# One decode block with its gradients on one core: w1 and w3 loaded first, two V buffers, seven output tiles, ScalarE's order written by hand

## The chip, the cores and the metric

The kernel runs on one core of a Trainium2 chip. The metric is the device time of one execution in microseconds (us), the median of the runs shown below. A profile is one execution recorded by the hardware profiler; its times are those of that execution. TensorE (PE) multiplies matrices, VectorE (DVE) and ScalarE (ACT) work elementwise, GpSimd (POOL) here issues the stores, SyncE (SP) the loads.

## The reference, cut to what matters

One token of a transformer block, forward and backward. The forward part is attention over a cache of 32 heads and a gated MLP, both on the same normalized row, and the kernel returns the output and the gradients for x, the K and V caches, wq, wo, w1, w3 and w2.

```python
# A: x (1,1,640), k_cache and v_cache (1,32,8192,128), wq (640,4096), wo (4096,640), all bf16
q = (xn @ wq).reshape(B, Sq, 32, 128).transpose(0, 2, 1, 3)
p = softmax(einsum("bhqd,bhkd->bhqk", q, k) * 128 ** -0.5)
o = einsum("bhqk,bhkd->bhqd", p, v)
attn = o.transpose(0, 2, 1, 3).reshape(B, Sq, 4096) @ wo
# B: w1, w3 (640,1728), w2 (1728,640)
mlp = (silu(xn @ w1) * (xn @ w3)) @ w2
out = x + attn + mlp                      # xn = layernorm(x)
# returned: out, and the gradients of sum(out * grad_out) for x, k_cache, v_cache, wq, wo, w1, w3, w2
```

A head's K and V are 8192 x 128 each, 2.10 MB; their gradients, which are outer products, are as large and are written out. Every input is read once and every gradient is written once: 151 MB each way.

## The kernel before

Heads are worked on one after the other, in groups of four (`GH`), of which there are eight (`NG`); wq is loaded for two groups at a time, wo for one. Before the heads comes the MLP, with its gradients. Each K or V of a head lies in SBUF as 128 partitions x 64 rows x 128 columns.

The order of the instructions on VectorE, SP and POOL is the order of the program (`ORDERED`). On TensorE and ScalarE a scheduler of the framework chooses it at build time. All loads of K, V and weights are issued on SP in program order, and a load waits there until its buffer is free, with all later loads behind it. All stores of large outputs are issued on POOL, again in order.

The start (lines 98 to 157): x and grad_out are loaded, then on SP the three pieces of w2, wq of the first pair of groups, wo of group 0, w1, w3, K of head 0, and V of heads 0, 1 and 2. w1 and w3 lie in buffers of K; there are three such buffers, so K of heads 1 and 2 can be loaded only after the gradients dw1 and dw3, which are written over w1 and w3, have been stored. The pieces of w2, two scratch tiles of the MLP (`diag`, `bc_sb`) and the output tiles `ot` share the pool `op` of five buffers.

`mlp_steps` (lines 415 to 503) first multiplies w2 by the gradient of the output (L427 to L423), and stops at a `yield`. Then `prep_steps(0)` runs for the first group. Then come gate and up (L441, 160 matmuls of one column), a chain of small operations on VectorE (L446 to L459), `diag` (L461), its spreading over all partitions (L470 to L476, `bc_sb`), the gradient of w2 on ScalarE (L485), the products with w1 and w3 for the gradient of x (L492, L495), and the gradients of w1 and w3 (L498), which are stored (L502).

The loop over heads works on two heads in one iteration: on head h (`c`), and on the scores of head h+1 (`n`). For n: `product(n, "S")`, K times q on VectorE (L312), summed on TensorE (L314), in two halves; `row_max`; `product(n, "DP")`, the same with V and the gradient of o; `exps`. For c: `probs`, `row_dots`, `attend` (V times probabilities on TensorE), `dscores` (with K on TensorE), and `outer`, four times: half of dV or dK. An output tile `ot` holds 32 rows of 128 columns for each partition, 1.05 MB in all; VectorE makes 24 of the rows (L321), ScalarE 8 (L325), and POOL stores the tile (L327).

`load_v(h + 3)` stands after `attend` of head h, and `load_k(h + 3)` after `dscores` of head h. In the first head of a group come `load_wq` (every second group) and `load_wo` for the next group. The buffer of `load_wo` is that of the group before, which has to be stored as dwo first.

`weights(c)` ends each head: `odq`, `om`, the transposes of this head's wq (L399) and the copy of them (L401), their product with dq (L403), and dq spread over the partitions (L406 to L409, into `dqbc`). At the last head of a group it calls `finish_wo` and `finish_wq`, which write the group's weight gradients over wo and wq on ScalarE (L273, four activations, and L279, five) and store them; some of the last groups' stores are kept in the list `late` until head 30.

`prep_steps(g)` makes q and the gradient of o for a group: five matmuls into `ps_q` and a scaled copy `qs_g` (L241), five times four transposes of wo (L248), a copy `woT` (L250) and a matmul (L252), and a copy `do_g` (L258). It is a generator; the loop calls `gap()` at set places, which runs the next part of the first generator in the list `steps`.

Of the kernel before, what the change touches and what calls it, by code (L numbers as in the profile page):

```python
# [9 lines left out]
BF16 = mybir.dt.bfloat16  # L10
# [6 lines left out]
P = 128  # L17
# [4 lines left out]
def kernel(  # L22
# [35 lines left out]
    ORDERED = {mybir.EngineType.DVE, mybir.EngineType.SP, mybir.EngineType.Pool}  # L58
# [9 lines left out]
    kvpool = ctx.enter_context(tc.tile_pool(name="kv", bufs=3))  # L68
# [3 lines left out]
    opool = ctx.enter_context(tc.tile_pool(name="op", bufs=5))  # L72
# [23 lines left out]
    with tc.manual_schedule(engines=ORDERED):  # L96
# [8 lines left out]
        def load_k(h):  # L105
            Kt = kvpool.tile([P, J, DH], BF16, name="Kt", tag="K")
            nc.sync.dma_start(Kt[:], kc[h])
            kv_tiles[h] = kv_tiles.get(h, [None, None])
            kv_tiles[h][0] = Kt

        def load_v(h):
            Vt = kvpool.tile([P, J, DH], BF16, name="Vt", tag="V")
# [26 lines left out]

        w2_parts = []  # L140
# [9 lines left out]
        w1t = kvpool.tile([P, NC, F], BF16, name="w1t", tag="K")  # L150
        nc.sync.dma_start(w1t[:], w1_v)
        w3t = kvpool.tile([P, NC, F], BF16, name="w3t", tag="K")
        nc.sync.dma_start(w3t[:], w3_v)
# [3 lines left out]
        load_v(2)  # L157
# [75 lines left out]
        def prep_steps(g):  # L233
            G_ = grp[g]
            wq_g, wo_g = G_["wq"], G_["wo"]
            ps_q = ps_w.tile([P, GH * DH], F32, name="ps_q", tag="w")
            for ci in range(NC):
                nc.tensor.matmul(ps_q[:], lhsT=XN_rep[:, ci, :], rhs=wq_g[:, ci, :],
                                 start=(ci == 0), stop=(ci == NC - 1))
            qs_g = wpool.tile([P, GH, DH], BF16, name="qs_g", tag="qs_g")  # L240
            nc.scalar.activation(qs_g[:].rearrange("p h d -> p (h d)"), ps_q[:], ACTF.Copy, scale=scale)  # L241
            G_["qs"] = qs_g
            ps_d = ps_w.tile([P, GH * DH], F32, name="ps_d", tag="w")
            for ci in range(NC + 1):
                if ci < NC:
                    ps_t = ps_w.tile([P, GH * DH], BF16, name="ps_t", tag="w")
                    for hh in range(GH):
                        nc.tensor.transpose(ps_t[:, hh * DH:(hh + 1) * DH], wo_g[:, hh, ci * P:(ci + 1) * P], ident_bf[:])  # L248
                    woT = wpool.tile([P, GH * DH], BF16, name="woT", tag="woT", bufs=2)
                    nc.scalar.copy(woT[:], ps_t[:])  # L250
                if ci > 0:
                    nc.tensor.matmul(ps_d[:], lhsT=G_rep[:, ci - 1, :], rhs=last[:],  # L252
                                     start=(ci == 1), stop=(ci == NC))
                last = woT
# [373 lines left out]
```

## Time and profile before

| | |
|---|---|
| median of the runs | 766.21 us |
| the runs | 764.54, 766.21, 769.57 us |
| the profiled execution | 767.92 us, of which its span is 765.8 us |
| busy: PE, DVE, ACT, POOL | 72%, 83%, 62%, 11% of the span |
| moved | 303.71 MB, half read and half written, mean 397 GB/s |
| granted TensorE clock, mean | 0.783 |

The span runs from the first instruction to the last event of the profile. A line of the waits says which engine and line waited for which; L312 is line 312 of the kernel before. "DMA share" is the mean busy share of the core's 16 DMA engines; it can read slightly above 1, since packets overlap. "out_dram<-ot" is the store of an output tile, "Kt<-in_A_k_cache_dram" the load of a K.

### The profile page before, as it was taken

To read this page: it belongs to the slowest core of one execution; us is meant where nothing else is said; L and a number is where in the kernel's file an instruction comes from. 1 tells how busy PE (TensorE), PEld (TensorE's weight loads), DVE (VectorE), ACT (ScalarE), POOL (GpSimd) and SP (SyncE) were. 2 spreads that over 40 slices of the span, in tenths; PEclk is the share of its full clock that TensorE was granted. 3 is DMA by queue.
4 is the path that set the end of the run, shared out by engine and by line. 5 is a ranking of instruction groups with operands and counts; after the bars stand their busy time and mean duration, and the time that the engine had idled before them with its cause. 6 is when DMAs were issued, how large, how long until landed. Compare 5 with 4: busy or idle time off the path is not lost.

```text
span 765.8 us, 15959 instructions
## 1 busy us (share of the span) xinstructions
PE 552.9 (72%) x6535; PEld 338.3 (44%) x6543; DVE 633.5 (83%) x706; ACT 473.2 (62%) x1421; POOL 81.9 (11%) x154
## 2 busy tenths in 40 slices
PE   5865689777766756878684764887775877787871
PEld 3753345443433433444353432554453444444450
DVE  6078899998987948999894976999896899899991
ACT  2261466776655836687573853877574686678665
POOL 0011011111101100011010110111110010011211
PEclk9657967977887877896796786977897878887885
DMA  8959799999999999999999999999999999999976
GB/s 283 423 226 328 303 409 427 425 427 417 428 428 428 412 414 395 392 403 424 426 427 429 381 414 424 354 428 423 418 426 429 405 412 427 426 425 421 412 317 247
DMA packets 37162, 303.71 MB, mean 397 GB/s; under 512 B 3928, under 2 KB 5682, under 8 KB 12002
## 3 DMA queue, kind: packets, MB, share of 16 engines
q0 software_dynamic: 21888, 151.35, 48.2%
q1 hardware_dynamic: 15190, 151.35, 48.0%
q8 instruction: 51, 0.84, 0.4%
q14 instruction: 21, 0.17, 0.1%
q10 hardware_dynamic: 12, 0.00, 0.0%
HBM read 151.34 MB, written 151.34 MB: 395 GB/s over the span
## 4 chain that ended last, share of the span: by engine, by line
DMA 40%; DVE 36%; issue 21%; POOL 2%; POOLq 0%; PE 0%; SPq 0%; DVEq 0%; ACT 0%
DMA out_dram<-ot 34%; DVE T L312 16%; DVE ot L321 14%; DMA Kt<-in_A_k_cache_dram 3%; DMA out_dram<-w1t 1%; DVE S_sb L331 1%; DVE DP_sb L365 1%; POOL out_dram L327 1%; DMA w2c<-in_B_w_dram 1%; DVE P L350 1%; POOL out_dram L124 1%; DVE U L373 1%; DVE junk L368 0%; DVE negM L340 0%; DVE mrow L333 0%
## 5 line engine op out<-in xcount | busy, mean ns | idle before, releaser
L314 PE MATMUL psDP<-T,ident_bf 128*128 128x512 bf16 x512 | 185.2, 524 | 68.4 <-DVE T L312 68.4
L314 PEld LDWEIGHTS <-ident_bf 128*128 128x128 bf16 x1024 | 118.0, 118 | 221.4 <-issue 165.4
L325 ACT ACTIVATE ot<-qs_g,Uf 128x128 bf16<-128x128 bf16 x512 | 154.5, 391 | 63.5 <-DMA out_dram<-ot 57.7
L325 ACT ACTIVATE ot<-do_g,Pf 128x128 bf16<-128x128 bf16 x512 | 156.3, 390 | 31.7 <-DMA out_dram<-ot 30.9
L312 DVE TENSOR_TENSOR T<-Kt,qs_g 128x4096 bf16<-128x4096 bf16 x64 | 146.4, 2289 | 2.3 <-DMA Kt<-in_A_k_cache_dram 1.8
L321 DVE TENSOR_TENSOR ot<-qs_g,U 128x3072 bf16<-128x3072 bf16 x64 | 112.2, 1754 | 42.5 <-DMA out_dram<-ot 42.3
L312 DVE TENSOR_TENSOR T<-Vt,do_g 128x4096 bf16<-128x4096 bf16 x64 | 146.0, 2282 | 0.0
L314 PE MATMUL psS<-T,ident_bf 128*128 128x512 bf16 x512 | 138.3, 417 | 10.4 <-DVE T L312 10.2
L321 DVE TENSOR_TENSOR ot<-do_g,P 128x3072 bf16<-128x3072 bf16 x64 | 112.4, 1756 | 28.4 <-DMA out_dram<-ot 27.2
L327 POOL DMA_DIRECT2D out_dram<-ot x128 | 68.2, 533 | 553.8 <-ACT ot L325 388.1
L378 PEld LDWEIGHTS <-Kt 128*128 128x128 bf16 x2048 | 57.6, 98 | 31.6 <-issue 27.6
L378 PE MATMUL ob<-U,Kt 128*128 128x1 bf16 x2048 | 56.9, 164 | 18.3 <-DVE U L373 18.1
L358 PEld LDWEIGHTS <-Vt 128*128 128x128 bf16 x2048 | 56.6, 97 | 0.0
L358 PE MATMUL ob<-P,Vt 128*128 128x1 bf16 x2048 | 55.9, 163 | 0.0
L335 PE MATMUL sm<-ident_f,mrow 128*128 128x128 f32 x64 | 19.4, 395 | 43.4 <-DVE mrow L333 43.2
L409 ACT CAST dqbc_g<-ps_db 128x128 bf16<-128x128 f32 x32 | 8.5, 265 | 54.2 <-PE ps_db L408 54.2
L390 ACT ACTIVATE om<-rmask,odq 128x4 f32<-128x4 f32 x32 | 9.4, 295 | 40.5 <-DVE odq L386 40.5
L344 PEld LDWEIGHTS sm<-rsum,ones_f 128*128 128x128 f32 x64 | 15.1, 259 | 41.6 <-ACT E L343 37.2
L335 PEld LDWEIGHTS sm<-ident_f,mrow 128*128 128x128 f32 x64 | 12.5, 240 | 46.6 <-DVE mrow L333 44.6
L343 ACT ACTIVATE E<-S_sb,negM 128x64 f32<-128x64 f32 x32 | 11.0, 344 | 35.6 <-DVE negM L340 35.6
L344 PE MATMUL sm<-rsum,ones_f 128*128 128x1 f32 x64 | 12.7, 268 | 18.7 <-ACT E L343 18.7
L279 ACT ACTIVATE wq_g<-dqbc_g,xn_col 128x512 bf16<-128x512 bf16 x40 | 26.0, 709 | 0.0
(145 smaller groups left out, 554.9 us busy)
## 6 DMA issues: line engine op xcount, KB each, us to landing
out_dram<-ot POOLq DMA_DIRECT2D x128, 1024.0 KB, 18.5
Kt<-in_A_k_cache_dram SPq DMA_DIRECT2D x32, 2048.0 KB, 15.7
Vt<-in_A_v_cache_dram SPq DMA_DIRECT2D x32, 2048.0 KB, 12.2
wq_g<-in_A_wq_dram SPq DMA_DIRECT2D x4, 1280.0 KB, 21.4
wo_g<-in_A_wo_dram SPq DMA_DIRECT2D x8, 640.0 KB, 16.0
out_dram<-wo_g POOLq DMA_DIRECT2D x8, 640.0 KB, 13.3
out_dram<-wq_g POOLq DMA_DIRECT2D x3, 1280.0 KB, 18.1
w1t<-in_B_w_dram SPq DMA_DIRECT2D x1, 2160.0 KB, 17.3
```

The costliest lines, as they stand in the source:

```text
L279: nc.scalar.activation(G_["wq"][:, ci, :], G_["dqbc"][:].rearrange("p h d -> p (h d)"), ACTF.Copy, scale=xn_col[:, ci:ci + 1])
L312: nc.vector.tensor_tensor(T[:], src[:, :, ds_], vec[:, ds_].unsqueeze(1).to_broadcast([P, J, DHH]), ALU.mult)
L314: nc.tensor.matmul(ps[:], lhsT=ident_bf[:], rhs=T[:, :, RUN * i:RUN * (i + 1)], start=(half == 0 and i == 0), stop=(half == 1 and i == DHH ...
L321: nc.vector.tensor_tensor(ot[:, 0:JD], vec.rearrange("p (a b) -> p a b", b=2).unsqueeze(1).to_broadcast([P, JD, DH // 2, 2]), w2[:, j0:j0 ...
L325: nc.scalar.activation(ot[:, j].rearrange("p a b -> p (a b)"), vec, ACTF.Copy, scale=wf[:, half, j - JD:j - JD + 1])
L327: nc.gpsimd.dma_start(dst[h][:, j0:j0 + JH, :], ot[:].rearrange("p j a b -> p j (a b)"))
L335: nc.tensor.matmul(st.sm[:, 8:8 + P], lhsT=mrow[:].to_broadcast([P, P]), rhs=ident_f[:], start=True, stop=True, skip_group_check=True)
L343: nc.scalar.activation(st.E[:], st.S[:], ACTF.Exp, bias=negM[:], scale=1.0, accum_out=rsum[:])
L344: nc.tensor.matmul(st.sm[:, 3:4], lhsT=ones_f[:], rhs=rsum[:], start=True, stop=True, skip_group_check=True)
L358: mm = nc.tensor.matmul(st.ob[:, 0:1], lhsT=st.V[:, j, :], rhs=st.P2[:, j, 0:1], start=(j == 0), stop=(j == J - 1), skip_group_check=True)
L378: nc.tensor.matmul(st.ob[:, 1:2], lhsT=st.K[:, j, :], rhs=st.U2[:, j, 0:1], start=(j == 0), stop=(j == J - 1), skip_group_check=True)
L390: nc.scalar.activation(om[:], rmask[:], ACTF.Copy, scale=odq[:, 0:1])
```

## The change

The loads of w1 and w3 move to the front of SP's queue, and gate and up to the front of the MLP; the place where the MLP stops for `prep_steps(0)` moves behind `diag`. K and V get pools of their own: three buffers for K, two for V, and V of head h+2 is loaded where V of head h+3 was. The pool of output tiles has seven buffers instead of five. ScalarE joins the engines whose order is that of the program. `finish_wo` and `finish_wq` become the generator `finish_steps`, whose four parts run in the four gaps of the next head; dwq of a pair of groups is stored in five parts. `prep_steps` is cut in more parts. From `weights`, the transposes of wq go to a place after `attend` (`turn_wq`), their copy behind the first half of dK (`keep_wq`), and the copy into `dqbc` to the next iteration (`keep_dq`).

```diff
-    ORDERED = {mybir.EngineType.DVE, mybir.EngineType.SP, mybir.EngineType.Pool}
+    ORDERED = {mybir.EngineType.DVE, mybir.EngineType.SP, mybir.EngineType.Pool, mybir.EngineType.Activation}
...
-    kvpool = ctx.enter_context(tc.tile_pool(name="kv", bufs=3))
+    kpool = ctx.enter_context(tc.tile_pool(name="kp", bufs=3))
+    vpool = ctx.enter_context(tc.tile_pool(name="vp", bufs=2))
...
-    opool = ctx.enter_context(tc.tile_pool(name="op", bufs=5))
+    opool = ctx.enter_context(tc.tile_pool(name="op", bufs=7))
...
+        w1t = kpool.tile([P, NC, F], BF16, name="w1t", tag="K")
+        nc.sync.dma_start(w1t[:], w1_v)
+        w3t = kpool.tile([P, NC, F], BF16, name="w3t", tag="K")
+        nc.sync.dma_start(w3t[:], w3_v)
         w2_parts = []
...
-        w1t = kvpool.tile([P, NC, F], BF16, name="w1t", tag="K")
-        nc.sync.dma_start(w1t[:], w1_v)
-        w3t = kvpool.tile([P, NC, F], BF16, name="w3t", tag="K")
-        nc.sync.dma_start(w3t[:], w3_v)
         load_k(0)
         load_v(0)
         load_v(1)
-        load_v(2)
...
+            def turn(ci):
+                ps_t = ps_w.tile([P, GH * DH], BF16, name="ps_t", tag="w")
+                for hh in range(GH):
+                    nc.tensor.transpose(ps_t[:, hh * DH:(hh + 1) * DH], wo_g[:, hh, ci * P:(ci + 1) * P], ident_bf[:])
+                return ps_t
+
+            def keep(ps_t):
+                woT = wpool.tile([P, GH * DH], BF16, name="woT", tag="woT", bufs=2)
+                nc.scalar.copy(woT[:], ps_t[:])
+                return woT
...
+            ps_t = turn(0)
+            yield
...
+            woT = keep(ps_t)
+            ps_t = turn(1)
+            yield
...
+            for ci in range(NC):
+                nc.tensor.matmul(ps_d[:], lhsT=G_rep[:, ci, :], rhs=woT[:], start=(ci == 0), stop=(ci == NC - 1))
+                if ci + 1 < NC:
+                    woT = keep(ps_t)
+                if ci + 2 < NC:
+                    ps_t = turn(ci + 2)
+                if ci + 1 < NC:
+                    yield
+            yield
...
-        def finish_wo(g):
+        def finish_steps(g):
...
+            for r in range(GH):
                 nc.scalar.activation(wo_g[:, r, :], g_bc_bf[:], ACTF.Copy, scale=on[:, r:r + 1])
+                if r == 1:
+                    yield
             store(dwo_v[g], wo_g[:], g == NG - 2)
+            yield
+            b, k = divmod(g, HB)
             for ci in range(NC):
                 nc.scalar.activation(G_["wq"][:, ci, :], G_["dqbc"][:].rearrange("p h d -> p (h d)"),
                                      ACTF.Copy, scale=xn_col[:, ci:ci + 1])
+                if g < NG - HB and k == HB - 1:
+                    store(dwq_v[:, ci, b * GW * DH:(b + 1) * GW * DH], G_["wq_all"][:, ci, :], g == NG - HB - 1)
+                if ci == 2:
+                    yield
...
+        def turn_wq(st):
+            st.ps_wqT = ps_w.tile([P, D], BF16, name="ps_wqT", tag="w")
...
+        def keep_wq(st):
+            st.wqT = small.tile([P, D], BF16, name="wqT", bufs=1)
+            nc.scalar.copy(st.wqT[:], st.ps_wqT[:])
...
+        def keep_dq(st):
+            G_, hh = st.G, st.hh
+            if hh == 0:
+                G_["dqbc"] = wpool.tile([P, GH, DH], BF16, name="dqbc_g", tag="dqbc_g", bufs=1)
+            nc.scalar.copy(G_["dqbc"][:, hh, :], st.ps_db[:])
             if hh == GH - 1:
...
+                steps.append(finish_steps(st.g))
...
                 outer(c, c.do, c.P2, c.Pf, dvc, h, 0)
+                if prev:
+                    keep_dq(prev)
                 gap()
                 row_dots(c)
                 attend(c)
+                turn_wq(c)
...
                 outer(c, c.do, c.P2, c.Pf, dvc, h, 1)
-                if h + 3 < H:
-                    load_v(h + 3)
+                if h + 2 < H:
+                    load_v(h + 2)
                 gap()
                 dscores(c)
                 outer(c, c.q, c.U2, c.Uf, dkc, h, 0)
+                keep_wq(c)
...
-                if hh == 2 and g + 1 < NG:
+                if hh == 2:
                     gap()
+            prev = c
+        keep_dq(prev)
         while steps:
             gap()
```

## The prediction

> **What bounds the kernel now.** I read first the page's slices, then windows of chosen length, then the chain and the waits, then the time line of the first 100 us and of the last 50.
>
> ```profile
> DMA  8959799999999999999999999999999999999976
> GB/s 283 423 226 328 303 409 427 425 427 417 428 428 428 412 414 395 392 403 424 426 427 429 381 414 424 354 428 423 418 426 429 405 412 427 426 425 421 412 317 247
> DMA packets 37162, 303.71 MB, mean 397 GB/s; under 512 B 3928, under 2 KB 5682, under 8 KB 12002
> ```
>
> A slice is 765.8 / 40 = 19.15 us. The transfers run at up to 428 GB/s, and 303.71 MB at that rate need 709.6 us, so 56 us of the span are lost to it. By slices: the first five (0 to 96 us) sum to 1563 of 2140, 1.35 slices, **25.8 us**; the next 33 have a mean of 416, **17.4 us**; the last two sum to 564 of 856, **13.1 us**. VectorE comes second: an undisturbed head takes it 18.75 us (starts of L312 at 83.62, 102.37 and 121.12 in the chain), while a head moves 4 x 2.10 MB of K, V, dK and dV and a quarter of a group's 2.62 MB of weights, 9.04 MB or 21.1 us. So in the middle the transfers set the pace and VectorE waits for output tiles. The waits, with us in total, times, longest:
>
> ```profile
> ACT ot L325 <- DMA out_dram<-ot: 88.6, 32, 5.1
> DVE ot L321 <- DMA out_dram<-ot: 69.5, 35, 6.2
> DVE T L312 <- DMA Kt<-in_A_k_cache_dram: 1.8, 1, 1.8
> ```
>
> Stores lag and loads run ahead: almost nobody waits for K or V. Then windows: start:end and length, busy us of PE, PEld, DVE, ACT, POOL (instructions), granted clock, DMA share, GB/s.
>
> ```profile
> 48.00:52.00 4.00, 4.00 (x70) 3.85 (x68) 2.13 (x2) 4.00 (x6) 0.00 (x0) 0.50 0.04 16
> 52.00:56.00 4.00, 3.89 (x43) 3.66 (x42) 3.65 (x2) 4.00 (x7) 1.06 (x1) 0.70 0.35 108
> ...
> 430.00:440.00 10.00, 8.48 (x147) 5.68 (x146) 9.90 (x12) 10.00 (x26) 1.91 (x3) 0.84 0.91 344
> 480.00:490.00 10.00, 9.30 (x173) 6.76 (x171) 9.93 (x9) 10.00 (x33) 1.60 (x3) 1.00 0.81 295
> ...
> 740.00:744.00 4.00, 3.54 (x60) 2.51 (x59) 3.94 (x5) 3.32 (x12) 0.16 (x1) 0.94 0.34 139
> 744.00:748.00 4.00, 2.48 (x96) 2.38 (x92) 3.97 (x5) 4.00 (x15) 0.90 (x2) 0.91 0.76 311
> ```
>
> Three kinds of hole. At 48 us all that can be loaded is loaded and nothing is ready to be stored. At 430 and 480 ScalarE is busy the whole window: a group's weight gradients (L273, L279) go before its parts of the output tiles, and stores come late. At 740 the loads are done, and VectorE alone makes 4.2 MB per 18.75 us, half of what the transfers can take. The first hole in the time line (start, length, engine and line; in brackets the idle time before):
>
> ```profile
> 24.12 3.71 PE L441 MATMUL gu_ps<-xn_col_bf,w1t 128*108 128x1 bf16 x38 [1.94 <-DMA w1t<-in_B_w_dram]
> 31.96 7.61 PE L441 MATMUL gu_ps<-xn_col_bf,w3t 128*108 128x1 bf16 x80
> 39.60 0.19 DVE L446 COPY sm_f<-gu_ps 108x32 f32<-108x32 f32 x1 [21.84 <-PE gu_ps L441]
> 46.30 3.83 DVE L492 TENSOR_TENSOR T<-w1t,bc_sb 128x3456 bf16<-128x3456 bf16 x2
> 60.66 0.57 POOL L502 DMA_DIRECT2D out_dram<-w1t  x1
> 71.94 7.72 SPq L107 DMA_DIRECT2D Kt<-in_A_k_cache_dram  x2
> 83.62 2.29 DVE L312 TENSOR_TENSOR T<-Kt,qs_g 128x4096 bf16<-128x4096 bf16 x1 [1.78 <-DMA Kt<-in_A_k_cache_dram]
> ```
>
> This is one chain: w1 lands at 24 us, gate and up take 15.4 us (3.71 + 4.04 + 7.61), VectorE waits for them 21.84 us, the products follow, dw1 is stored, and only then is w1's buffer free for K of head 1, without which head 0 can't go on.
>
> The profiled execution took 767.92 us for a span of 765.8; the median of 766.21 is 1.7 lower. I sum changes of the span and take them off the median.
>
> **1. w1 and w3 first.** Each is 2.21 MB, 5.2 us at 428 GB/s. From the first w2 issue (1.14) and x's 1.55 us from issue to landing, w1 is there at about 8 us and w3 at 13. w2's second piece was used 2.5 us after the first (9.95 against 7.49), 276 GB/s, so its three pieces now land by about 21.5. Gate and up, if they take 15.4 us as before, end at 23.5. The w2 part follows on TensorE: 4.95 + 1.56 us of L430 and a reduction of 0.49, to 30.5. The copy of gate and up (39.60) moves by **-9**. Bounds: if TensorE mixes the two, the last w2 piece decides, 21.5 + 1.8 + 1.6 + 0.5 = 25.4, or -14; if L430 too runs at half the clock, 6.5 us more, or -2.6. That TensorE's order isn't written by hand is why both stay open.
>
> The clock row bears on this: L441 ran with 0.50 granted throughout 24 to 40 us, while 0 to 20 had 1.00, so I keep the measured 15.4. The Trainium skill (TensorE: Matmul & The Clock Gate, "Part 1: The HAM clock gate") says that the clock is released after some 3.4 us of sustained work; here 15 us of one-column multiplies didn't release it. By the rule they would take about half, and 4 us more would be gained.
>
> **2. The hand-written order at the start.** ScalarE now does the preparation of group 0 (one scaled copy 0.60, five woT at 0.58, do_g 1.29; 17.34 to 23.8 in the trace with TensorE between, 6.5 us) ahead of the copies of bc_sb. VectorE's small operations and diag cover 4.3 us (39.60 to 43.9). Loss **+2.2**; 0 if it is done during gate and up, 6.5 if nothing covers it. So L492 starts at 39.5 instead of 46.3, and dw1's store, K1 and head 0 come 7 us earlier.
>
> **3. One V fewer ahead.** Four loads of K and V instead of five before the heads: 2.10 MB, **4.9 us** of transfers, go from the start into the stream. The hole at 48 us then begins 4.9 earlier and ends 7 earlier. The start gains **2.1**; from -8 (7 more from part 1's better end, less 1) to +5.
>
> **4. Does V still come in time?** load_v(h+2) is issued about 7.5 us into head h (91.13 against 83.62), when attend has freed the buffer. DP of head h+2 needs it 12.2 us into head h+1 (95.84 against 83.62): 18.75 + 12.2 - 7.5 = 23.4 us. V lands in 12.2 (median), 26.5 at most. Cost **0**, with 11 us to spare. On SP's queue stands load_wo before it once a group, and that waits for the store of the older dwo (five waits, 54.0 us, longest 15.0). dwo now goes out some 5 us later in the next head (after 16 copies of ot and four of 0.8), so V of one head per group may be issued 10 us later. With the median landing it still comes 1.2 us early, with K's median (15.7) 2.3 late, halfway to V's longest (19.4) 6 late; while VectorE waits, the tiles in the queue keep the transfers busy. Bounds 0 and, at 4 us for each of 7 groups, 28; I take 0, since before the change only one K and no V was waited for.
>
> **5. Seven output tiles, gradients in parts.** The middle dips below full share at 300 (0.89), 430 (0.91), 480 (0.81), each 10 us long, and a little at 320 and 600: 1.1 + 0.9 + 1.9 + 0.4 = 4.3 us. Shorter ScalarE bursts and two more tiles of 1.05 MB should close most: **-3**, bounds 0 and -4.3. The remaining 13 us of the middle are full share at fewer GB/s, and stay. What moves costs ScalarE nothing as long as it isn't the bound: the head after a group now holds 32 parts at 0.305 (eight take 2.44), wo 3.0, wq 3.3 and small ones of 2.9, 19.0 us, under 21.1.
>
> dwq of a pair of groups goes out in five stores instead of one. POOL starts stores 2.33 us apart when they queue up (440.42, 442.76, 445.09), so five take 11.7 us, twice, and delay the next head's first store (5.6 us into it) by 3 to 6 us; two or more tiles of 2.45 us each lie ahead in the queue and cover that. Without that cover: +12. A third set goes out with the late stores at head 30.
>
> The Trainium skill (DMA: Bandwidth & Descriptors, "Anatomy of one DMA") speaks against this: 2.0 us for each transfer plus its bytes at 436 GB/s, and half efficiency at 860 KB. By it five stores of 0.26 MB take 13 us and one of 1.31 MB takes 5: three times 8 us lost, a time near 778, if they ran alone. In the trace stores and loads overlap, the share being 0.99 where those three stores were issued, so I follow the row.
>
> **6. The end.** Loads now finish about a head later than the compute needs (V of head 31 is issued in head 29, not 28), and up to seven tiles stand in the queue when head 30 starts at 720.7, where before it had drained. The holes from 728 to 752 (410, 326, 139, 311, 401 GB/s and so on) make 5.4 us and those of 752 to 760 another 3.3; the last gradients and their landing (750.8 to 765.8) stay as they are. I take **-7**; 0 and -8.7 are the bounds.
>
> Sum: -2.1 - 3 - 7 = -12.1. 766.2 - 12.1 = **754 us**.
>
> **Rivals.** *Hidden anyway:* the transfers are saturated in the middle, the tail is a fixed chain, and the earlier start is eaten by the missing V: -2.1 and perhaps -2, 762 to 764. For it: the share of 1.0 nearly everywhere from 96 to 728. Against: the holes at the end are real.
>
> *V late (slower):* the third V buffer was what kept VectorE from waiting for loads. Behind load_wo and the longer store queue, V of one or two heads per group comes after its 23.4 us and every later instruction of VectorE waits. For it: the longest landing is 26.5 us, and the load ahead of it waits up to 15.0. Against: reads then pause, so stores drain at full rate and free what is waited for. It decides once the queue of output tiles runs dry, that is, beyond some 7 x 2.45 = 17 us without a new store. At the bound of 28 us: 754 + 28 = 782.
>
> *The edit doesn't do what it says:* TensorE is still ordered by the scheduler, and gate and up may not go first; the start gains nothing, and with +5 for the missing V it is 766.2 + 5 - 10 = 761. *More than forecast:* TensorE mixes the first products, -8 - 4.3 - 8.7 = -21, 745.
>
> **How the numbers follow.** Forecast (746 to 758.5) 0.56; more than forecast 0.10; hidden or undone (758.5 to 774) 0.17; V late 0.17. One per cent, 7.7 us, is about what a measurement of this kernel tells from no change. Faster: 0.66; within: 0.17; slower: 0.17. The range goes from 740 (the bounds of the gains, and a little for the run) to 775, which leaves out most of the V case.
>
> **What would show it.** Right: the copy at L446's place near 30 us, the first K product of head 1 near 76, no DMA share under 0.95 at group ends, stores still dense when head 31 starts, a V wait near 0. Wrong: VectorE's T waiting for Vt, ScalarE's exponent waited for in heads after a group, or a DMA hole in 736 to 748 as deep as before.

## The result, and the profile after

The changed kernel takes 761.22 us (median of eight runs, 760.47 to 762.55), the kernel before in the same comparison 766.81 (764.54 to 770.11): a ratio of 0.9924, with a 95% interval of 0.9904 to 0.9943. That is a gain of 5.6 us where 12.1 were forecast. The profiled execution took 761.41 us for a span of 759.4.

The page of the changed kernel, slices of 759.4 / 40 = 18.99 us:

```profile
DMA  8969799999999999999999999999999999999795
GB/s 298 335 258 366 301 428 425 423 422 418 430 427 428 423 416 426 426 423 417 429 428 426 426 377 430 424 427 419 430 425 427 428 418 427 428 427 424 325 363 201
DMA packets 37355, 303.72 MB, mean 400 GB/s; under 512 B 4120, under 2 KB 5874, under 8 KB 12194
```

The middle is now dense: one slice below 416 from the sixth to the 37th. But the last three read 325, 363 and 201, where before only the last two were low. To put a number on each part, cut both spans at two events: the first product of K in the iteration that works on head 0's gradients (the change's 78.11 us, before 83.62), and the same place for head 30 (706.89, before 720.69). The windows of the kernel before, then of the changed one (start:end and length, busy us of PE, PEld, DVE, ACT, POOL, granted clock, DMA share, GB/s):

```profile
0.00:83.62 83.62, 55.73 (x482) 42.41 (x484) 46.87 (x62) 24.92 (x39) 5.22 (x13) 0.76 0.85 320
83.62:720.69 637.07, 474.02 (x5694) 280.38 (x5700) 557.68 (x600) 418.53 (x1293) 70.27 (x131) 0.79 1.00 414
720.69:765.80 45.11, 23.17 (x361) 15.48 (x359) 28.89 (x45) 29.70 (x90) 6.38 (x11) 0.72 0.77 300
```

```profile
0.00:78.11 78.11, 53.51 (x474) 41.36 (x476) 46.77 (x63) 24.18 (x38) 5.22 (x13) 0.88 0.89 317
78.11:706.89 628.78, 479.07 (x5695) 280.02 (x5710) 556.88 (x601) 420.47 (x1294) 73.08 (x137) 0.79 1.00 420
706.89:759.40 52.51, 24.73 (x361) 15.93 (x359) 28.86 (x45) 29.70 (x90) 9.17 (x16) 0.63 0.75 287
```

Length less bytes at 428 GB/s is what a part loses (bytes: GB/s times length, by the packet records). Before: 21.1 us in the start, 21.5 in the middle, 13.6 at the end. After: 20.3, 12.2 and 17.3. So the start gained 0.8 us (2.1 forecast), the middle 9.3 (3 forecast), and the end **lost** 3.7 (7 were to be gained). The end is where the forecast failed.

The waits that answer to those shown of before (us in total, times, longest):

```profile
ACT ot L346 <- DMA out_dram<-ot: 68.4, 30, 13.0
...
DVE ot L342 <- DMA out_dram<-ot: 43.9, 24, 10.5
...
POOL out_dram L125 <- DMA out_dram<-ot: 30.4, 11, 6.9
...
DVE T L459 <- DMA w2c<-in_B_w_dram: 15.8, 3, 12.2
...
DVE T L333 <- DMA Vt<-in_A_v_cache_dram: 1.4, 1, 1.4
```

VectorE and ScalarE wait less for output tiles (43.9 and 68.4 us against 69.5 and 88.6), and V is waited for once, 1.4 us. New is the third line: POOL, which issues the stores, waits for stores to land before it can issue the next; the waits of the kernel before have no such line. The windows where the forecast looked for holes:

```profile
44.00:48.00 4.00, 4.00 (x42) 3.89 (x40) 2.36 (x3) 4.00 (x7) 1.06 (x1) 0.71 0.38 160
...
440.00:450.00 10.00, 6.20 (x51) 3.40 (x48) 9.62 (x10) 6.40 (x21) 2.16 (x4) 0.66 0.90 341
480.00:490.00 10.00, 10.00 (x126) 5.96 (x124) 9.79 (x12) 6.66 (x22) 0.59 (x2) 0.84 1.01 423
...
714.00:718.00 4.00, 3.79 (x51) 2.07 (x49) 3.96 (x5) 1.94 (x8) 0.73 (x2) 0.67 0.54 211
718.00:722.00 4.00, 2.47 (x46) 1.79 (x43) 3.97 (x5) 4.00 (x13) 0.81 (x2) 0.50 0.51 206
722.00:726.00 4.00, 3.72 (x13) 1.68 (x11) 3.86 (x7) 0.96 (x5) 1.87 (x4) 0.55 0.61 220
...
748.00:752.00 4.00, 0.00 (x0) 0.00 (x0) 0.00 (x0) 0.00 (x0) 0.00 (x0) 0.50 0.70 205
```

At 480 the hole at the end of a group is gone (share 1.01, before 0.81); the one at 430 has moved to 440 (0.90, before 0.91). The hole of the start stands at 44 us, and a new one has opened from 714 to 726, when head 31 is still to be worked on and VectorE is busy nearly all the time. From 748 on no engine works and the last stores drain. POOL's own time line shows what happens in that new hole (start, length, operation; in brackets the idle time before and what ended it):

```profile
704.85 0.53 POOL L348 DMA_DIRECT2D out_dram<-ot  x1 [3.69 <-ACT ot L346]
705.37 0.55 POOL L125 DMA_DIRECT2D out_dram<-wq_g  x1
708.47 0.55 POOL L125 DMA_DIRECT2D out_dram<-wq_g  x1 [2.56 <-DMA out_dram<-ot]
711.05 0.54 POOL L125 DMA_DIRECT2D out_dram<-wq_g  x1 [2.03 <-DMA out_dram<-ot]
...
721.73 0.82 POOL L125 DMA_DIRECT2D out_dram<-wq_g  x1 [2.06 <-DMA out_dram<-ot]
724.51 1.80 POOL L348 DMA_DIRECT2D out_dram<-ot  x3 [1.95 <-DMA out_dram<-ot]
```

The same stores in the kernel before:

```profile
719.18 0.86 POOL L124 DMA_DIRECT2D out_dram<-wq_g  x1
719.86 0.72 POOL L124 DMA_DIRECT2D out_dram<-wo_g  x1
720.39 1.04 POOL L124 DMA_DIRECT2D out_dram<-wq_g  x1
```

The seven late stores (five of dwq, one of dwo, one of dwq) go out 2.6 to 3.1 us apart instead of 0.6. Six of them leave 0.3 us after a landing (708.19 us and 708.47, 710.77 and 711.05, 713.37 and 713.65), and it is always the landing of the store eight places before. POOL's stores use eight semaphores in turn, so at most eight are on the way. Before, with five output tiles, there were never more than six on the way, and the three late stores left within 1.2 us. Behind the late stores stand head 30's output tiles: the first could go at 724.51 only, and three left within 1.8 us.

The places are short earlier too. In the changed kernel 34 of POOL's 158 stores were issued 0.3 to 0.6 us after the store eight before had landed, 24 of them between 100 and 700 us; in the kernel before none was. The five stores of dwq at 430.10, 437.56, 440.84, 443.50 and 446.00 us are among them, and they are what stands at the dip of 440 to 450.

The start (line by line, for the chain that the prediction followed):

```profile
9.47 7.62 PE L448 MATMUL gu_ps<-xn_col_bf,w1t 128*108 128x1 bf16 x80 [3.68 <-DMA w1t<-in_B_w_dram]
16.96 7.61 PE L448 MATMUL gu_ps<-xn_col_bf,w3t 128*108 128x1 bf16 x80
19.70 2.16 DVE L459 TENSOR_TENSOR T<-w2c,g_bc_bf 108x3840 bf16<-108x3840 bf16 x1 [12.15 <-DMA w2c<-in_B_w_dram]
...
29.09 1.83 DVE L459 TENSOR_TENSOR T<-w2c,g_bc_bf 108x3200 bf16<-108x3200 bf16 x1 [0.65 <-DMA w2c<-in_B_w_dram]
32.94 0.18 DVE L471 COPY sm_f<-gu_ps 108x32 f32<-108x32 f32 x1
40.42 3.82 DVE L518 TENSOR_TENSOR T<-w1t,bc_sb 128x3456 bf16<-128x3456 bf16 x2
54.74 0.57 POOL L528 DMA_DIRECT2D out_dram<-w1t  x1
66.06 7.99 SPq L108 DMA_DIRECT2D Kt<-in_A_k_cache_dram  x2
78.11 2.29 DVE L333 TENSOR_TENSOR T<-Kt,qs_g 128x4096 bf16<-128x4096 bf16 x1 [1.26 <-PE psDP L335]
```

Gate and up do go first and are over at 24.57. The copy comes 6.7 us earlier than before (32.94 against 39.60), the product of w1 5.9 earlier, K of head 1 5.9 earlier and head 0's first product 5.5 earlier. What sets the copy is now the last piece of w2, at 29.09.

### The profile page after: what moved, and what is told of

It reads as the page before. It is cut to its first block, busy times and chain, and to the rows that moved or that the text cites. A ratio compares the mean times of both kernels' runs of the same rounds, so it can differ in the third digit from the quotient of the medians.

```text
span 759.4 us, 15976 instructions
## 1 busy us (share of the span) xinstructions
PE 557.3 (73%) x6528; PEld 337.3 (44%) x6543; DVE 632.5 (83%) x706; ACT 474.4 (62%) x1421; POOL 87.5 (12%) x166
## 4 chain that ended last, share of the span: by engine, by line
DMA 55%; DVE 31%; PE 6%; issue 4%; ACT 2%; SPq 1%; POOL 0%; POOLq 0%; DVEq 0%; ACTq 0%
DMA out_dram<-ot 39%; DVE T L333 14%; DVE ot L342 11%; DMA out_dram<-wo_g 9%; DMA wo_g<-in_A_wo_dram 4%; DMA w2c<-in_B_w_dram 3%; PE psS L335 2%; ACT ot L346 1%; DVE S_sb L352 1%; DVE DP_sb L386 1%; PE psDP L335 1%; PE dx_ps L521 1%; DVE w3t L524 1%; DVE T L518 1%; SPq L149 0%
## 5 line engine op out<-in xcount | busy, mean ns | idle before, releaser
L335 PE MATMUL psDP<-T,ident_bf 128*128 128x512 bf16 x512 | 187.2, 529 | 65.3 <-DVE T L333 65.3
L335 PEld LDWEIGHTS <-ident_bf 128*128 128x128 bf16 x1024 | 120.2, 120 | 221.8 <-issue 167.0
L346 ACT ACTIVATE ot<-qs_g,Uf 128x128 bf16<-128x128 bf16 x512 | 156.4, 389 | 68.6 <-DMA out_dram<-ot 55.9
L335 PE MATMUL psS<-T,ident_bf 128*128 128x512 bf16 x512 | 141.2, 426 | 9.4 <-DVE T L333 9.4
L245 ACT COPY woT<-ps_t 128x512 bf16<-128x512 bf16 x40 | 22.8, 576 | 25.9 <-PE ps_t L240 25.9
L418 ACT ACTIVATE dq_diag<-ident_bf,odq 128x128 bf16<-128x128 bf16 x32 | 12.8, 399 | 41.2 <-DVE odq L414 41.2
L356 PE MATMUL sm<-ident_f,mrow 128*128 128x128 f32 x64 | 17.6, 361 | 23.8 <-DVE mrow L354 23.0
L373 ACT ACTIVATE Pf<-E,rZ 128x16 f32<-128x16 f32 x32 | 9.8, 307 | 39.2 <-DVE rZ L369 39.2
L352 DVE TENSOR_REDUCE S_sb<-psS 128x64 f32<-128x512 f32 x32 | 21.9, 685 | 11.2 <-PE psS L335 11.2
L262 PE MATMUL ps_d<-woT,G_rep 128*128 128x512 bf16 x33 | 13.4, 405 | 22.6 <-ACT woT L245 22.6
```

The lines of the kernel that those rows point to most:

```text
L262: nc.tensor.matmul(ps_d[:], lhsT=G_rep[:, ci, :], rhs=woT[:], start=(ci == 0), stop=(ci == NC - 1))
L335: nc.tensor.matmul(ps[:], lhsT=ident_bf[:], rhs=T[:, :, RUN * i:RUN * (i + 1)], start=(half == 0 and i == 0), stop=(half == 1 and i == DHH ...
L346: nc.scalar.activation(ot[:, j].rearrange("p a b -> p (a b)"), vec, ACTF.Copy, scale=wf[:, half, j - JD:j - JD + 1])
L352: nc.vector.tensor_reduce(st.S[:], st.ps["S"][:], AX.X, ALU.add)
L356: nc.tensor.matmul(st.sm[:, 8:8 + P], lhsT=mrow[:].to_broadcast([P, P]), rhs=ident_f[:], start=True, stop=True, skip_group_check=True)
```

## The experiments

All ratios are to the kernel before, run beside them (its medians there lay between 766.8 and 768.5 us, so small differences are read from the ratios). For reading them together, this is what each profiled execution lost by the measure above (us; "sum" is span less 303.7 MB at 428 GB/s, within rounding). A row is one execution, which can lie off the median of its kernel's runs: 765.07 against 762.35 for the new start alone, 761.79 against 760.31 for the last dwq in one store.

| kernel | start | middle | end | sum |
|---|---|---|---|---|
| before | 21.1 | 21.5 | 13.6 | 56.2 |
| before, new start alone | 15.6 | 24.0 | 13.7 | 53.3 |
| changed | 20.3 | 12.2 | 17.3 | 49.8 |
| changed, old start | 24.6 | 12.4 | 17.0 | 54.0 |
| changed, five output tiles | 20.1 | 17.9 | 13.6 | 51.6 |
| changed, five tiles and three V | 16.2 | 19.0 | 14.6 | 49.8 |
| changed, ScalarE by the scheduler | 20.5 | 12.7 | 16.2 | 49.4 |
| changed, last dwq in one store | 20.7 | 12.9 | 16.6 | 50.2 |
| the same, two loads earlier | 15.2 | 12.7 | 16.6 | 44.5 |
| changed, half the column multiplies | 19.1 | 10.6 | 13.8 | 43.5 |
| the same, wide multiplies instead | 18.4 | 11.8 | 14.4 | 44.6 |
| changed, dscores twice | 19.2 | 15.8 | 18.0 | 53.0 |
| changed, wide multiplies added | 19.6 | 13.5 | 18.4 | 51.5 |
| two loads earlier, w2 in longer pieces | 38.2 | 11.7 | 16.1 | 66.0 |

**The last pair's dwq in one store.** Does the new hole cost what it looks like?

```diff
-                if g < NG - HB and k == HB - 1:
-                    store(dwq_v[:, ci, b * GW * DH:(b + 1) * GW * DH], G_["wq_all"][:, ci, :], g == NG - HB - 1)
+                if g < NG - HB - 1 and k == HB - 1:
+                    store(dwq_v[:, ci, b * GW * DH:(b + 1) * GW * DH], G_["wq_all"][:, ci, :])
+                if g == NG - HB - 1 and ci == NC - 1:
+                    store(dwq_v[:, :, b * GW * DH:(b + 1) * GW * DH], G_["wq_all"][:], True)
```

> The changed kernel with one edit: the dwq of the last pair of groups that is kept for head 30 is one store of 1.31 MB again, not five of 0.26 MB; the other pairs stay in five. Theory 'places': POOL has eight stores on their way at most, each new one waits until the store eight before it has landed, and the small stores hold places that the 1.05 MB tiles of head 30 need; with three late stores instead of seven the first tile of head 30 goes out near 712 and not at 724.5, the DMA share in 710 to 726 goes from 0.5-0.6 to over 0.9, and the time falls by 4 to 7 us, to 755-757. Rival 'production': the hole at the end is there because the loads are done and VectorE alone makes 4.2 MB in 18.75 us, so the time stays at 760.5-762 and the hole only moves.

Measured: 760.31 us (758.75 to 761.79), ratio 0.9914 [0.989, 0.9937]. Windows of this kernel:

```profile
714.00:718.00 4.00, 4.00 (x78) 2.81 (x76) 4.00 (x3) 2.26 (x8) 0.55 (x1) 1.00 1.01 410
...
726.00:734.00 8.00, 6.55 (x152) 5.27 (x152) 7.75 (x13) 6.80 (x24) 1.06 (x2) 0.93 0.80 330
742.00:746.00 4.00, 0.21 (x1) 0.00 (x0) 1.03 (x5) 4.00 (x7) 0.53 (x1) 0.50 0.52 195
...
750.00:754.00 4.00, 0.00 (x0) 0.00 (x0) 0.00 (x0) 0.00 (x0) 0.00 (x0) 0.50 0.07 29
```

The split stores made the hole: it is closed, and head 30's first tile leaves at 714.77 instead of 724.51. But only 0.9 us came of it, which the two intervals don't tell from nothing. The rest went into new holes behind: 726 to 734 at 0.80, and a tail from 750 in which a share of 0.07, about one sixteenth, remains at 29 GB/s. One of the 16 DMA engines is still at work, one 8-KB packet after another at some 309 ns. The trace shows it in the store's semaphore, which is raised 16 times for each store (the Trainium skill, DMA: Bandwidth & Descriptors, "Why a DMA increments its semaphore by 16 and not by 1", says that it is once for each engine, and that only the full count means that all has landed). In this run, time of the first, 15th and 16th raise (the reports of the engines) of four stores:

```
issued   1st     15th    16th     16th - 15th
707.44   715.63  719.76  727.99   8.2
718.35   723.81  727.80  736.81   9.0
730.73   734.72  735.13  744.43   9.3
738.49   742.73  743.98  753.39   9.4
```

Fifteen engines are done and one is 8 to 9 us behind. The mean over all 128 stores of output tiles is 1.2 us in the kernel before (no 100-us stretch above 2.1), 5.4 in the changed one (11.5 from 600 to 700 us) and 7.1 here. In the changed kernel the same lag holds the eight places longer: the store issued at 704.85 had 15 raises by 716.15 and the last at 723.93, and the one whose landing let the second late store go had 15 by 696.72 and the last at 708.19.

**Five output tiles, and the old buffers.**

```diff
-    vpool = ctx.enter_context(tc.tile_pool(name="vp", bufs=2))
+    vpool = ctx.enter_context(tc.tile_pool(name="vp", bufs=3))
-    opool = ctx.enter_context(tc.tile_pool(name="op", bufs=7))
+    opool = ctx.enter_context(tc.tile_pool(name="op", bufs=5))
...
-                if h + 2 < H:
-                    load_v(h + 2)
+                if h + 3 < H:
+                    load_v(h + 3)
```

The first kernel has the second of these edits alone, the other one all of them and `load_v(2)` in the start.

> The changed kernel with five output tiles instead of seven, all else the same (two V buffers). Theory 'buffers': the 9 us that the middle of the run gained (416 to 425 GB/s) come from the two more output tiles, which keep the store queue full over ScalarE's bursts; without them the middle is back at 414-418 GB/s and the time is 768-772. Rival 'parts': the gain comes from the shorter ScalarE bursts, and with five tiles the time stays within 2 us of 761. Third: fewer tiles queued means shorter landings for dwo, so loads of wo wait less, and it is even faster, 757-760.

> The changed kernel with the buffers of before: three V buffers, V of head 2 loaded at the start, load_v(h+3), five output tiles. Theory 'buffers': as op5, the middle loses most of its gain, time 765-768. Rival 'parts': ScalarE's order and the gradients in parts did it, time 757-761, the holes at 430 and 480 of the kernel before stay closed.

Measured: 762.96 us (761.54 to 763.17), ratio 0.9944 [0.9925, 0.9964], and 761.22 (760.03 to 762.52), 0.9928 [0.9903, 0.9954]. The second is the changed kernel's time with the old buffers, so by the times 'parts' came nearer than 'buffers'. The table shows what buffers do: two more tiles take 5.7 us out of the middle and put 3.7 into the end, and the third V takes 4 out of the start and puts 2 back. The sums lie within 2 us of each other. With five tiles the lag is smaller (3.6 and 3.4 us on average) and fewer stores had to wait for a place (17 and 13), but both are well above the kernel before with its five tiles (1.2 us, none).

**ScalarE's order by the scheduler.** `Activation` is taken out of `ORDERED` again.

> The changed kernel with ScalarE's order chosen by the scheduler again. If the order by hand matters in the middle, the scheduler pulls the gradients of wo and wq ahead of the output tiles' parts in some heads and the time is 763-766; if it matters only at the start (preparation ahead of the copies of bc_sb, 2 us), 759-761.

Measured: 761.57 us (759.49 to 762.65), ratio 0.9929 [0.9905, 0.9953], no difference from the changed kernel. The hand-written order is worth nothing that these runs can tell.

**The start by itself, both ways.** The moved loads of w1 and w3, the moved multiplies of gate and up and the moved `yield`, undone in the changed kernel and made alone in the one before.

```diff
+        w1t = kvpool.tile([P, NC, F], BF16, name="w1t", tag="K")
+        nc.sync.dma_start(w1t[:], w1_v)
+        w3t = kvpool.tile([P, NC, F], BF16, name="w3t", tag="K")
+        nc.sync.dma_start(w3t[:], w3_v)
         w2_parts = []
...
             bc_sb = opool.tile([P, 2, F], BF16, name="bc_sb", tag="o")
+            yield
```

> The changed kernel with the start of before: w1 and w3 loaded after w2, wq and wo, gate and up after the w2 part, the stop for group 0's preparation before gate and up. All else as changed. Theory 'start': the five runs so far (changed, one late store, five tiles, three V, ScalarE free) lie within 3 us of each other, so buffers, order and parts are worth little, and the whole gain is the heads starting 5.5 us earlier (78.1 against 83.6); then this one is at 765-768, no faster than before. Rival 'stream': the middle's gain is real and adds up with the start, and this one is at 761-764.

> The kernel before with the start of the change alone: w1 and w3 first, gate and up first, the stop moved behind diag. Theory 'start': 760-763, the whole gain of the change. Rival 'stream': 763-766, since the stream of heads stays at 414 GB/s.

Measured: without the new start 766.1 us (764.39 to 767.51), ratio 0.9986 [0.997, 1.0003]; with it alone 762.35 (761.11 to 765.22), 0.994 [0.9918, 0.9962]. So nearly the whole gain is the start. Everything else together, which is most of the diff, gives 1 us, not told from nothing. In the table the start alone saves 5.5 us; the same start with one V fewer ahead saves 0.8. Of the 4.7 between the two most is the 2.10 MB of that V: the two kernels with five tiles, which differ in the V buffer and that load alone, start at 20.1 and 16.2, 3.9 apart.

**Where does the lag come from?** The page lists a queue of instructions, 51 packets of 16 KB in the changed kernel: 0.84 MB, which is 64 bytes for each of TensorE's 13,071 multiplies and weight loads. The kernel before has the same 51. First, fewer and more multiplies: attend and dscores take every second row (`for j in range(0, J, 2)`), or dscores is done a second time into a column that nobody reads. With half the rows left out the gradients of wq and wo aren't the reference's; those of K and V are.

> The changed kernel without every second of the 64 one-column multiplies of attend and of dscores (each a weight load and a multiply; the sums leave out half the rows). That is 128 TensorE instructions a head less, 4096 in all, about a third of TensorE's stream. Theory 'one transfer engine': in the changed kernel one of the 16 transfer engines finishes each store later than the other 15 (11.5 us on average between 600 and 700 us, 1 to 2 us before the change); it is the one that also fetches TensorE's instructions, 51 packets of 16 KB that the page shows as kind instruction, 0.84 MB. With a third fewer of them the lag of the last engine falls below 5 us and the time falls by 5 to 10 us, to 751-756. Rival 'other cause': the lag is a property of the engine or of the weights' shapes, the transfers carry the same data, and the time stays within 2 us of 761 (TensorE, at 73% busy, isn't the bound).

> The changed kernel with dscores' 64 one-column multiplies done a second time into an unused column: 128 TensorE instructions a head more, 4096 in all, about 16 more packets of 16 KB of instructions and 1.74 us more of TensorE's time a head (73% to about 81% busy). Theory 'one transfer engine': the lag of the last engine grows and the time rises by 5 to 10 us, to 766-771. Rival 'other cause': TensorE has room and the time stays within 2 us of 761.

Measured: 755.32 us (754.52 to 755.94), ratio 0.9849 [0.9822, 0.9876], and 764.52 (763.84 to 765.6), 0.9969 [0.9953, 0.9984]: the first as 'one transfer engine' had it, the second between the two answers. TensorE was busy 73% of the span in the changed kernel, yet 2048 multiplies with their weight loads move the time by -5.9 and +3.3 us. Time on TensorE and number of instructions changed together, so a run with four 512-column multiplies more per head and few instructions followed.

```diff
+            st.junk = ps_w.tile([P, 4, DH], F32, name="ps_junk", tag="w")
+            for i in range(4):
+                nc.tensor.matmul(st.junk[:], lhsT=ident_bf[:], rhs=st.K[:, 4 * i:4 * i + 4, :], start=(i == 0), stop=(i == 3))
```

> The changed kernel with TensorE time added without many instructions: after dscores four multiplies of 512 columns a head into a PSUM tile that nobody reads, 8 instructions a head (256 in all, one more packet of 16 KB) and some 1.7 us of TensorE a head at half the clock, as much as the 64 one-column multiplies of the run with dscores done twice, which took 764.5. Theory 'one transfer engine' (what counts is the instructions fetched): within 1.5 us of 761. Rival 'TensorE's time': 763.5-766, as that run. If it is in between, both count.

Measured: 762.69 us (761.78 to 763.19), ratio 0.9937 [0.9918, 0.9957], 1.5 more than the changed kernel (1.0 by the ratios) for 20 us more of TensorE and one packet. That settles little: the intervals overlap, and TensorE's busy time rose by 20 us where the run with dscores twice has 55 more. A better test is half the column multiplies with eight such wide ones per head in their place (the last diff with `range(8)`).

> The kernel leaves out every second multiply of attend and of dscores (so its gradients of K, V and the weights of attention aren't the reference's), and gives the time on TensorE back with eight 512-column multiplies per head whose sum nobody reads. TensorE should again be busy some 555 us, as in the changed kernel (557.3), while its instructions stay near those of the run with half the multiplies: about 39 packets of instructions instead of 51 (there 35). Theory A, the packets of TensorE's instructions hold up one of the 16 DMA engines: 16 packets fewer were worth 5.9 us, so 12 fewer give 4.4 us: about 757 us, and the last of a store's 16 reports stays as close behind the fifteenth as with half the multiplies (3.4 us on average, 5.4 in the changed kernel). Theory B, the time on TensorE itself is what cost the 5.9 us: about 761 us, with 5 to 6 us between the last two reports. 759 would tell nothing.

Measured: **755.66 us** (755.25 to 756.42), ratio 0.9844 [0.9819, 0.9869]. The pages of the run with half the multiplies and of this one:

```profile
PE 514.9 (68%) x4480; PEld 289.8 (39%) x4495; DVE 633.0 (84%) x706; ACT 474.3 (63%) x1421; POOL 87.5 (12%) x166
...
q8 instruction: 35, 0.57, 0.3%
```

```profile
PE 544.3 (72%) x4751; PEld 305.3 (41%) x4751; DVE 632.4 (84%) x706; ACT 473.7 (63%) x1421; POOL 87.5 (12%) x166
...
q8 instruction: 37, 0.61, 0.3%
```

29 us more on TensorE cost nothing that can be told: 0.3 us by the medians, none by the ratios (0.9844 against 0.9849). TensorE came to 544 instead of the 555 that were aimed at; at 5.9 us for the 42.4 us between 557.3 and 514.9, time on TensorE would have given 755.3 + 5.9 * 29.4 / 42.4 = 759.4. So it isn't TensorE's time in all. What the two fast kernels have in common is 14 to 16 packets fewer, worth 5.6 to 5.9 us or about 0.4 us each, where 16 KB at one engine's share (428 / 16 = 26.75 GB/s) would take 0.61; 16 packets more cost 3.3 us, 0.2 each. That fits one engine which carries its sixteenth of the data and the instructions besides. While the lag is still growing it goes with the packets too: for the tiles issued from 300 to 400 us its mean is 2.2 us with 35 packets, 3.4 with 37, 3.8 to 7.2 in the kernels with seven tiles and 51 or 52, and 9.3 with 67.

Three things stand against calling it shown. Both fast kernels also have an attend of half the length (31 us of TensorE in all instead of 57), which frees V's buffer for the next load sooner; no run separates that from the instructions. Of their gain, 1.2 and 1.9 us lie in the start by the table, before any of these multiplies has run, and the run with more of them starts as early (19.2). And over the whole program the lag is no gauge of the time: 3.4 us with half the multiplies, but 4.6 here, where 3.4 was expected to stay; 3.6 in the kernel with five tiles, which takes 762.96, and 6.0 in the next one, which takes 756.22. Which engine a packet ran on isn't in the trace. That fewer instructions help by way of the lagging engine is therefore likely, not shown.

**Two loads earlier.** If all 16 engines had more to do in the hole at 44 us, the rest of the program would have less. On top of the single store, `load_wo(1)` and `load_wq(1)` go to the end of the start's loads.

```diff
         load_v(1)
+        load_wo(1)
+        load_wq(1)
...
-                    if (g + 1) % HB == 0:
+                    if (g + 1) % HB == 0 and g > 1:
                         load_wq((g + 1) // HB)
-                    load_wo(g + 1)
+                    if g > 0:
+                        load_wo(g + 1)
```

> The changed kernel with dwq of the last pair kept as one store, and with wo of group 1 and wq of groups 2 and 3 (0.66 and 1.31 MB) loaded at the end of the loads of the start, not in heads 0 and 4. The hole between 42 and 58 us (DMA share 0.17 to 0.67) has nothing to load; 1.97 MB are 4.6 us of transfers. Theory 'all transfers count' (the stream is bound by transfers from the first head to the last): 756-758. Rival 'the start of the heads sets it' (what counts is when head 0 starts, which doesn't move): 760-761.

Measured: 756.22 us (755.22 to 756.64), ratio 0.9857 [0.9832, 0.9883]: 4.1 less than the single store alone, and the best version that computes everything. Its windows:

```profile
46.00:48.00 2.00, 2.00 (x19) 1.94 (x17) 1.28 (x2) 2.00 (x4) 0.79 (x1) 0.61 0.06 25
48.00:52.00 4.00, 1.69 (x30) 1.57 (x28) 4.00 (x1) 4.00 (x7) 1.23 (x2) 1.00 0.59 197
```

```profile
46.00:48.00 2.00, 2.00 (x23) 1.94 (x22) 1.97 (x2) 2.00 (x4) 0.96 (x1) 0.73 0.76 281
48.00:52.00 4.00, 0.77 (x18) 0.65 (x16) 4.00 (x2) 4.00 (x7) 0.96 (x1) 1.00 0.85 320
```

The first two lines are the kernel with the single store alone, the second two this one. The share of 46 to 48 us rises from 0.06 to 0.76; the start's loss falls by 5.5 us, the middle's and the end's stay, and the time falls by 4.1. Here no later part took the gain back.

**w2 in longer pieces.** w2 was loaded with 16 neighbouring rows per partition, so that each packet is longer, which makes the slices of w1 and w3 and the writes of `bc_sb` strided.

```diff
-    w2_v = B_w2.rearrange("(r q) c -> q r c", r=R2)
+    w2_v = B_w2.rearrange("(q r) c -> q r c", r=R2)
...
-                        nc.tensor.matmul(gu_ps[0:FR, wi, r:r + 1], lhsT=wt[:, ci, r * FR:(r + 1) * FR],
+                        nc.tensor.matmul(gu_ps[0:FR, wi, r:r + 1], lhsT=wt[:, ci, :].rearrange("p (q r) -> p r q", r=R2)[:, r, :],
```

> As the run before, and w2 and its gradient taken as 108 partitions x 16 neighbouring rows, so that a partition's share of a piece is one run of 6.4 to 7.7 KB and not five or six of 1.25 KB; columns of w1 and w3 are taken with a stride of 16 for gate and up. In the changed kernel the pieces of w2 were waited for until 29.09 us, 8 us later than predicted. If the short runs did that, the copy of gate and up moves from 33 to about 27 us, head 0 with it, and the time falls by 4 to 6 us more, to 751-754; if TensorE's gate and up (9.5 to 24.6) or the 12 of 16 transfer engines decide, by 0 to 2.

Measured: 777.36 us (777.09 to 777.81), ratio 1.0135 [1.0109, 1.0161]: slower, not faster. Two of its groups (busy us, mean ns):

```profile
L452 PE MATMUL gu_ps<-xn_col_bf,w3t 128*108 128x1 bf16 x80 | 16.2, 340 | 0.0
...
L506 ACT CAST bc_sb<-bc_ps 128x432 bf16<-128x432 f32 x6 | 11.4, 2337 | 0.0
```

The first piece of w2 was used no earlier (20.35 us, 19.70 in the changed kernel), the second 0.9 us earlier (24.03, 24.89), gate and up took 16.2 us each instead of 7.6, and the copies into `bc_sb` on ScalarE 11.4 us instead of 2.9. The strides cost more than the transfer could have given.

## Why the prediction was right or wrong, step by step

The direction was right; the gain was less than half of the forecast, because **step 6, the end,** had the wrong sign: 3.7 us lost where 7 were to be gained. The start gained 1.3 us less than forecast and the middle 6.3 more, and the sum is -0.8 - 9.3 + 3.7 = -6.4, the difference of the spans.

- **1, w1 and w3 first.** The copy moved by 6.7 us, not 9. Gate and up took 15.2 us (15.4 assumed) and began at 9.47. The mis-sized term was w2: its last piece was used at 29.09, not 21.5. w1 landed at 9.43 and w3 at 15.57 us, not 8 and 13, and from 13 to 25 us the transfers moved 208 to 239 GB/s, where 276 had been taken for w2. From there on the working holds (1.83 + 1.52 + 0.49 give 32.9). The reason given for 15.4 was wrong, though: the granted clock was 1.00 from 0 to 20 us and still 80 of these multiplies took 7.6 us, as at 0.50 before. The Trainium skill (TensorE: Matmul & The Clock Gate, "Part 1: The HAM clock gate") shows multiplies of 128 columns that take about half the time once the clock is released. For one-column multiplies with a weight load each, these rows show no such gain.
- **2, the order at the start.** The product of w1 followed the copy after 7.48 us instead of 6.70: a loss of 0.8, not 2.2. With the 2.3 missing from step 1, head 0 came 5.5 us earlier, not 7.
- **3, one V fewer ahead.** Right: 4.7 us by the two starts of the table, 3.9 by the pair that differs in V alone (4.9 predicted). It eats the gain of the start, all but 0.8.
- **4, V in time.** Right: 1.4 us of waiting once, although SP now waits 145.1 us in all for the store of dwo (before 54.0; the longest wait 25.5). The rival *V late* didn't come, and the rival that the edit does nothing fell with gate and up at 9.47 and the copy at 32.94.
- **5, seven tiles and gradients in parts.** The middle gained 9.3 us, not 3. Part of the 13 us "at fewer GB/s", which the prediction left alone, could be won too: with five tiles, but the gradients in parts, the middle loses 17.9, and seven tiles make it 12.2. For the split stores the prediction read 2.33 us between stores as POOL's own pace. It was the pace of ScalarE: the rows of 442.76 and 445.09 name its part of the tile (L325) as what POOL waited for, and its eight parts of a tile take about 2.4 us. Where places are free, POOL's stores leave 0.5 to 0.7 us apart. What does hold the split stores back is the limit of eight places. An estimate by the rule of the Trainium skill that was weighed there (DMA: Bandwidth & Descriptors, "Anatomy of one DMA": 2.0 us per transfer besides its bytes) was 24 us for three sets of split stores. The one set that was tried both ways cost 0.9, not told from nothing. "A third set goes out with the late stores" had been left without a price, and it was that set that filled the eight places.
- **6, the end.** Assumed: two heads of fixed work, and seven tiles in the queue at their start "where before it had drained". It hadn't: before, six stores of 5.8 MB together were on the way when head 30 started at 720.69; after, seven tiles and one small store, 7.6 MB, at 706.89. So the queue was 1.8 MB fuller, and it was stuck: the late stores took the places one landing at a time, and each of these landings came 7 to 11 us after the other 15 engines had reported. The end's loss comes with the seven tiles: 13.6 with five, as before the change, and 17.3 with seven. With seven the last dwq in one store closes the hole at 714 to 726, and the loss moves into later holes and a tail of one engine (16.6). A reading that fits all these rows, argued and not shown: with five tiles the other engines soon have to wait for the slow one and the loss lies in the middle; with seven they run ahead, and the loss waits at the end.

*The edit doesn't do what it says* gave 761, the measured time, and that is luck: gate and up did go first, and the start and the 10 us that it kept for the middle and the end came out otherwise. *Hidden anyway* came next (762 to 764): its missing V was right, but the middle could still give 9 us, and the end took 4 back.

Of the signs named beforehand, head 1's product (78.11, near 76 expected) and the V wait held, and the copy missed by 3 us. "No DMA share under 0.95 at group ends" held at 480 and failed at 440 (0.90), where the split stores waited for places. "Stores still dense when head 31 starts" failed: the deep hole came, only earlier, at 714 to 726.

Left open: which engine fetches the instructions, whether the lag is that fetch alone, and why the lag is 3.4 us or more with five tiles in the changed kernel and 1.2 in the kernel before.

## What to carry to other kernels

Where the transfers are the bound, count what each part of the span loses against their full rate, and ask of every planned gain whether it lowers the sum. Here two more tiles took 5.7 us out of the middle and put 3.7 into the end, and one V fewer ahead put about 4 into the start; what shortened the time was to give the engines work earlier, and to leave out multiplies. Before you price a hole, see what would be late next: compare the last of a store's 16 reports with the fifteenth, and count how many stores are on the way when late ones are added to the queue. More buffers help little where the stores that empty them wait for a place.

## What the runs showed of the hardware

- POOL's stores rotate over eight semaphores; the ninth waits for the first to land in full (issues 2.6 to 3.1 us apart from 705 to 725 us, 0.5 to 0.7 where places are free; 34 of 158 stores of the changed kernel waited so, none before).
- A store lands when its last of 16 reports comes, and that can be 8 to 9 us after the fifteenth (8.2 to 9.4 for the stores issued from 707 to 739 us in the single-store kernel).
- TensorE's instructions are transfers too: 64 bytes each, 51 packets of 16 KB. Two kernels with 14 and 16 packets fewer were 5.6 and 5.9 us faster, with TensorE busy 72% and 68% of the span; that the packets are the reason isn't shown.
- 80 one-column multiplies, each with a weight load of 108 columns, took 7.61 us at a granted clock of 0.50 and 7.62 at 1.00.
- A weight load of 108 columns with a stride of 32 bytes takes 298 ns where 217 were seen without it, and a VectorE copy of 128x432 written with that stride 2.1 us against 0.61.
